# A recurrent attention with two feed-forward blocks on one core: a unit pattern made on chip, key loads of 48 rows, the last block's products in two parts, and another rank table

## The chip, the core and the metric

The kernel runs on one core of a Trainium2 chip. The time is device microseconds of one launch, from the core's own records. A change is called faster or slower here if the time moves by more than 2%.

## The reference

An attention with a recurrent 40x40 state for each of 4 x 8 heads over 768 steps, then two feed-forward blocks on its output (3072 tokens of 320 numbers). All is float32, and the kernel keeps float32 accuracy by taking most operands apart into a high and a low part.

```
for t in range(768):                       # for each batch b and head h
    y[t]  = r[t] @ state
    Sa    = state @ a[t]
    state = state * w[t] - outer(Sa, b[t]) + outer(v[t], k[t])
x = y as [3072, 320]
x = maximum(x @ w1, x @ w2, x @ w3) @ w_out        # inner width 768
x = ((x @ w_a) * (x @ w_b)) @ w_out2               # inner width 1536
```

## The kernel before

**Stages.** The 768 steps are cut into 24 chunks of 32 steps. In a chunk the recurrence becomes products of small matrices and one triangular solve. Two chunks make a pair, 12 pairs p in all. For each pair there are four pieces of work:

- prep(p) loads the decays (tile Wp), the keys k and b (KT) and a (ZL), makes running products of the decays by scans on VectorE (L484, L488), scales KT and ZL by them (L492, L504), multiplies them (L535 or L517), masks the product (L542), and writes it to memory (BD). From there it comes back in another layout (BU), the solve (L602, L603) builds the inverse in the tile TX of TXp, and TX goes out and comes back (TD, TT, L570 and L574).
- chain(c), one for each chunk, carries the state from chunk to chunk. In order: L723, the three or four small products L737, L750, L756 and L764, the new state L790 and L795, then the transposes L697 and the next chunk's L723. Beside it L680, L838 and L856 make the output y, which goes into XY.
- gather(p) writes XY to memory (XD, L870) and loads it as columns (xf, L875 and L877).
- moe_a(p) is the first feed-forward block on the 256 tokens of the pair (L964, L989 to L993). It needs xf and all first weights. Its results go to memory.

The first weights are loaded by weights_a in six blocks m, each of two raw loads (wraw, L897, 768 KB and 512 KB). VectorE turns the raw numbers into floats (L887 to L890). For m below 3 TensorE then makes the low parts (L917, L918, L920); these come in 18 groups of three steps. moe_b(n), six blocks of 512 tokens, is the second feed-forward block: for each of 12 slices ff there are two products of eight matmuls (L1111), a copy, a multiplication and a split into a high part bgh and a low part bgl (L1128 to L1132), and three products into each of four banks (L1119 to L1121). After the last slice the banks are copied out (L1139, L1141) and stored.

**What sets the order.** The kernel records each operation with the data that it reads and writes, and Plan.run lists them: at every step it takes the engine that can go on first and on it, of those that could start within 0.05 us, the operation of the least rank. It has estimated durations of its own. The rank is the operation's `pri`, less 0.04 times the length of the work behind it, plus a number out of the table RANK, which has one for each stage (c0 is the chain of chunk 0, p3 is prep(3), m, l, w and g the blocks, the weights and the gathers) and engine. So the table moves whole groups of operations on each engine. The order that comes out is fixed in the program: each engine runs its list in that order, and an instruction that waits holds all behind it. SP's list holds nearly all transfers. Where the plan leaves TensorE a gap of more than about 0.3 us it puts in 128x128 matmuls of a constant that nobody reads (L360, called fillers here; each is two instructions).

**What the change touches.** setup() zeroes tiles on VectorE and GpSimd at the start, and loads TXp, in which each 32-column row of TX begins with a row of a unit matrix, from an input `eye` of 128 x 528 (L439). load() in prep fills KT: for pairs 0 and 1 from a padded input `kb0` in pieces of 128 rows (L454), for the other ten with two loads of 48 rows each, at partitions 0 and 64 (L458). KT has two buffers, and later loads leave the padding rows alone.

Of the kernel before, what the change touches and what calls it, by code (L numbers as in the profile page):

```python
# [15 lines left out]
B, H, S, D = 4, 8, 768, 40  # L16
# [4 lines left out]
DM, DFF, DFF2 = 320, 768, 1536  # L21
NT = B * S
# [300 lines left out]
def body(nc, tc, ia, out_ap):  # L323
# [5 lines left out]
    op = P.op  # L329
# [90 lines left out]
    def setup():  # L420
# [18 lines left out]
        dma(lambda w_: SP.dma_start(TXp, ia["eye"]), 270e3, w=["TX"], pri=-0.55)  # L439


    def prep(p):
# [6 lines left out]
        def load(tile, name, n, nb, w, c0, c1):  # L449

            nb = nb * (c1 - c0) // 2
            if p < n:
                src = ia[name + "0"][p].rearrange("p (c f) -> p c f", c=2)
                dma(lambda w_: SP.dma_start(tile[:, c0:c1], src[:, c0:c1]), nb * 128, w=w(0) + w(1), pri=pr)  # L454
                return
            for g in range(2):
                src = ia[name][p, g].rearrange("p (c f) -> p c f", c=2)
                dma(lambda w_, g=g, src=src: SP.dma_start(tile[GP[g]:GP[g] + 48, c0:c1], src[:, c0:c1]), nb * 48, w=w(g), pri=pr)  # L458
# [852 lines left out]
def layout(d):  # L1311
# [18 lines left out]
    for n, m in (("kb", 2),):  # L1330
        z = np.zeros((m, 2, 64, o[n].shape[-1]), f)
        z[:, :, 0:D] = o[n][0:m]
        o[n + "0"] = z.reshape(m, 128, -1)
# [57 lines left out]
```

## Time and profile before

| | |
|---|---|
| median of 3 runs | 1036.34 us (1031.04 to 1044.56) |
| the profiled execution | 1038.84 us, its span 1037.1 us |
| TensorE busy | 1009.8 us, 97% of the span |
| VectorE, ScalarE, GpSimd busy | 627.5, 511.2, 125.7 us |
| transfers | 97.31 MB, 94 GB/s over the span |
| mean granted TensorE clock | 0.988 of full |

The span runs from the first to the last instruction of the profiled execution, and 1.7 us of its time lie outside. TensorE is the engine that is nearly always busy, but fillers count as busy too, so its share says nothing on how much of its work is wanted. The table of stretches has the busy time of each engine in 20 us, the clock that TensorE was granted as a share of full speed, and what the transfers moved. A piece of the chain of waits is what ended last at that time.

### The profile page before, as it was taken

To read this page: it belongs to the slowest core of one execution; us is meant where nothing else is said; L and a number is where in the kernel's file an instruction comes from. 1 tells how busy PE (TensorE), PEld (TensorE's weight loads), DVE (VectorE), ACT (ScalarE), POOL (GpSimd) and SP (SyncE) were. 2 spreads that over 40 slices of the span, in tenths; PEclk is the share of its full clock that TensorE was granted. 3 is DMA by queue.
4 is the path that set the end of the run, shared out by engine and by line. 5 is a ranking of instruction groups with operands and counts; after the bars stand their busy time and mean duration, and the time that the engine had idled before them with its cause. 6 is when DMAs were issued, how large, how long until landed. Compare 5 with 4: busy or idle time off the path is not lost.

```text
span 1037.1 us, 34548 instructions
## 1 busy us (share of the span) xinstructions
PE 1009.8 (97%) x15104; PEld 911.3 (88%) x15104; DVE 627.5 (61%) x1091; ACT 511.2 (49%) x1179; POOL 125.7 (12%) x128
## 2 busy tenths in 40 slices
PE   8999799999999999899999999999999999999997
PEld 8787698989999899899989999888888888888886
DVE  6787668968777788777866587773232232322222
ACT  4336668676786767667767244342232222322221
POOL 3100235205012123032111000000000000000000
PEclk9889999999999999999999999999999999999999
DMA  8946468575557457655463324312020000000000
GB/s 235 174 111 155 103 161 180 117 168 111 121 138 142 94 122 155 140 132 104 117 161 109 95 85 130 97 54 72 1 57 1 1 26 1 26 1 1 26 1 28
DMA packets 156397, 97.31 MB, mean 94 GB/s; under 512 B 120912, under 2 KB 135376, under 8 KB 155280
## 3 DMA queue, kind: packets, MB, share of 16 engines
q1 hardware_dynamic: 156096, 94.88, 38.7%
q8 instruction: 120, 1.97, 0.8%
q14 instruction: 37, 0.30, 0.1%
q10 hardware_dynamic: 144, 0.16, 0.0%
HBM read 76.26 MB, written 18.74 MB: 92 GB/s over the span
## 4 chain that ended last, share of the span: by engine, by line
PE 94%; DMA 2%; issue 2%; SPq 1%; DVE 1%; ACT 0%; POOL 0%; DVEq 0%
PE bank L1111 26%; PE bank L964 20%; PE bank L360 4%; PE bank L1120 4%; PE bank L1121 4%; PE bank L1119 4%; PE bank L856 3%; PE bank L838 2%; PE bank L989 2%; PE bank L723 2%; PE bank L737 2%; PE bank L680 2%; PE bank L790 2%; PE bank L535 2%; PE bank L990 2%
## 5 line engine op out<-in xcount | busy, mean ns | idle before, releaser
L1129 DVE TENSOR_TENSOR bas<-bank,bas 128x512 f32<-128x512 f32 x72 | 49.8, 691 | 195.5 <-PE bank L1111 187.3
L1131 ACT ACTIVATE bgh<-bas 128x512 fp32r<-128x512 f32 x72 | 45.5, 632 | 144.5 <-DVE bas L1129 144.5
L1128 ACT ACTIVATE bas<-bank 128x512 f32<-128x512 f32 x72 | 43.1, 598 | 121.6 <-PE bank L1111 121.6
L964 PE MATMUL bank<-xhi,whi 128*128 128x256 f32 x432 | 95.5, 303 | 0.0
L1111 PE MATMUL bank<-bxhi,bw 128*128 128x512 f32 x336 | 91.3, 393 | 0.0
L964 PE MATMUL bank<-xhi,wlo 128*128 128x256 f32 x432 | 87.1, 283 | 0.0
L964 PE MATMUL bank<-xlo,whi 128*128 128x256 f32 x432 | 86.9, 283 | 0.0
L1132 DVE TENSOR_TENSOR bgl<-bas,bgh 128x512 fp32r<-128x512 f32 x72 | 49.8, 692 | 42.5 <-ACT bgh L1131 42.3
L1111 PEld LDWEIGHTS bank<-bxhi,bw 128*128 128x128 f32 x336 | 61.9, 188 | 11.9
L964 PEld LDWEIGHTS bank<-xhi,whi 128*128 128x128 f32 x432 | 66.5, 191 | 3.3
L360 PE MATMUL bank<-con 128*128 128x128 f32 x442 | 65.4, 302 | 3.9 <-DMA con<-in_con_dram 3.0
L964 PEld LDWEIGHTS bank<-xhi,wlo 128*128 128x128 f32 x432 | 67.4, 191 | 0.1
L964 PEld LDWEIGHTS bank<-xlo,whi 128*128 128x128 f32 x432 | 67.2, 191 | 0.0
L1111 PE MATMUL bank<-bxhi,be 128*128 128x512 f32 x240 | 65.6, 395 | 0.0
L979 DVE TENSOR_TENSOR hm<-bank,hm 128x512 f32<-128x512 f32 x72 | 49.5, 688 | 26.1 <-PE bank L964 20.7
L360 PEld LDWEIGHTS bank<-con 128*128 128x128 f32 x442 | 59.4, 212 | 6.4 <-ACT bank L432 2.9
L964 PE MATMUL bank<-xt,wt 128*128 128x256 f32 x216 | 61.1, 283 | 0.0
L964 PE MATMUL bank<-xl,wt 128*128 128x256 f32 x216 | 60.8, 282 | 0.0
L780 ACT ACTIVATE XX<-bank 32x320 f32<-32x320 f32 x96 | 41.1, 429 | 23.3 <-PE bank L750 15.1
L1111 PE MATMUL bank<-bxlo,bw 128*128 128x512 f32 x168 | 52.4, 393 | 0.0
L1111 PEld LDWEIGHTS bank<-bxhi,be 128*128 128x128 f32 x240 | 44.2, 188 | 9.0
L1121 PE MATMUL bank<-bo,bgl 128*128 128x320 f32 x168 | 51.8, 309 | 0.0
(201 smaller groups left out, 2555.8 us busy)
## 6 DMA issues: line engine op xcount, KB each, us to landing
KT<-in_kb_dram SPq DMA_DIRECT2D x20, 384.0 KB
wraw<-in_wpa_dram SPq DMA_DIRECT2D x6, 768.0 KB
Wp<-in_wf_dram SPq DMA_DIRECT2D x20, 198.4 KB
ZR<-in_vz_dram SPq DMA_DIRECT2D x48, 80.0 KB
XX<-in_vx_dram SPq DMA_DIRECT2D x48, 80.0 KB
XT<-in_vt_dram SPq DMA_DIRECT2D x24, 160.0 KB
RB<-in_rb_dram SPq DMA_DIRECT2D x48, 80.0 KB
YL<-in_ry_dram SPq DMA_DIRECT2D x48, 80.0 KB
```

The costliest lines, as they stand in the source:

```text
L360: P.keep = lambda b: T.matmul(bank[b][:, 0:128], ident, ident, start=True, stop=True)
L780: own.append(op("ACT", ac(320), lambda w_, o_=o_, i_=i_: A.activation(o_(), i_(w_), AF.Copy), r=[pu], w=[("XXu", x, pq)], pri=pr))
L964: T.matmul(ps, w, x, start=(i == 0), stop=(i == 7))
L979: op("DVE", dv(512, True), lambda w_, pn=pn: V.tensor_tensor(f(hm), bank[w_[pn]], f(hm), ALU.max), r=[pn], w=["hm"], fin=[pn], pri=ep)
L1111: T.matmul(ps, w, x, start=(k == 0), stop=(k == 7))
L1119: T.matmul(o, gh[:, c], oh, start=ff == 0, stop=False)
L1120: T.matmul(o, gh[:, c], ol, start=False, stop=False)
L1121: T.matmul(o, gl[:, c], oh, start=False, stop=ff == 11)
L1128: op("ACT", ac(512), lambda w_, j=j, pa=pa: A.activation(tb["as", j], bank[w_[pa]], AF.Copy), r=[pa], w=[("bas", j)], fin=[pa], pri=ep)
L1129: op("DVE", dv(512, True), lambda w_, j=j, pb=pb: V.tensor_tensor(tb["as", j], bank[w_[pb]], tb["as", j], ALU.mult), r=[pb], w=[("bas", j) ...
L1131: op("ACT", ac(512), lambda w_, j=j, k=k: A.activation(tb["gh", k], tb["as", j], AF.Copy), r=[("bas", j)], w=[("gh", k)], pri=ep)
L1132: op("DVE", dv(512), lambda w_, j=j, k=k: V.tensor_tensor(tb["gl", k], tb["as", j], tb["gh", k], ALU.subtract), r=[("bas", j), ("gh", k)], ...
```

## The change

- setup() no longer loads `eye`: GpSimd zeroes TXp and writes ones over its diagonal with a stride of 33. Four new memsets on VectorE zero the two KT buffers, 128 x 1024 each.
- prep(0) and prep(1) load KT as the others do: eight pieces of 48 rows in place of four of 128.
- In moe_b the products of the very last slice are recorded as five operations: first those of bgh into all four banks, and then those of bgl one bank at a time.
- All numbers of RANK are others, so the order of everything moves.

```diff
 RANK = {
-    "ACT": 0.30, "DVE": -2.07, "POOL": 4.13, "SP": -3.60, "c0ACT": 6.38, "c0DVE": 3.21, "c0PE": -0.34, "c0SP": 6.32,
...
+    "ACT": -1.43, "DVE": 5.20, "POOL": -0.79, "SP": -5.70, "c0ACT": 3.50, "c0PE": -2.32, "c0SP": 5.63, "c10ACT": 6.01,
...
 }
...
-        dma(lambda w_: SP.dma_start(TXp, ia["eye"]), 270e3, w=["TX"], pri=-0.55)
+        zero(TXp, ["TX"], "POOL", pri=-2)
+        diag = TXp[:, 16:17]
+        op("POOL", 0.2, lambda w_: G.memset(bass.AP(tensor=diag.tensor, offset=diag.offset, ap=[list(diag.ap[0]), [33, 16]]), 1.0), w=["TX"], pri=-2)
+        for i in R2:
+            for c in R2:
+                op("DVE", 1.1, lambda w_, i=i, c=c: V.memset(KT[i][:, c].rearrange("p u x k s -> p (u x k s)"), 0.0), w=[(k, i, c, g) for k in ("K", "Kc") for g in R2], pri=-5.0 + i + 0.5 * c)
...
-        def load(tile, name, n, nb, w, c0, c1):
+        def load(tile, name, nb, w, c0, c1):
 
             nb = nb * (c1 - c0) // 2
-            if p < n:
-                src = ia[name + "0"][p].rearrange("p (c f) -> p c f", c=2)
-                dma(lambda w_: SP.dma_start(tile[:, c0:c1], src[:, c0:c1]), nb * 128, w=w(0) + w(1), pri=pr)
-                return
             for g in range(2):
                 src = ia[name][p, g].rearrange("p (c f) -> p c f", c=2)
                 dma(lambda w_, g=g, src=src: SP.dma_start(tile[GP[g]:GP[g] + 48, c0:c1], src[:, c0:c1]), nb * 48, w=w(g), pri=pr)
...
+            if n == NT // 512 - 1 and ff == 11:
+                def front(w_, k=k, ff=ff):
+                    for t in range(4):
+                        for q in range(2):
+                            T.matmul(bank[w_[po_[t]]][:, 0:DM], tb["gh", k][:, t * 128:t * 128 + 128], wb("bo", ff)[:, q], start=False, stop=False)
+
+                op("PE", 1.17, front, r=[("gh", k), ("bL", ff, 1)], w=po_, pri=pr)
+                for t in range(4):
+                    op("PE", 0.146, lambda w_, t=t, k=k, ff=ff: T.matmul(bank[w_[po_[t]]][:, 0:DM], tb["gl", k][:, t * 128:t * 128 + 128], wb("bo", ff)[:, 0], start=False, stop=True),
+                       r=[("gl", k), ("bL", ff, 1)], w=[po_[t]], pri=pr)
+                continue
```

The changed file has one line more from L483 on, so L897 before is L898 there, and L1121 is L1122.

**SP, the first transfers.** KT_119 and KT_120 are the two buffers of KT, and ZL_121, ZL_122 and ZL_123 are ZL of pairs 0, 1 and 2; wraw is raw first weights. Before:

```order
L427 DMA con<-in_con_dram 128x224
L439 DMA TXp<-in_eye_dram 128x528
L463 DMA Wp<-in_wf_dram 64x529 x4
L454 DMA KT_119<-in_kb_dram 128x1024 x2
L471 DMA ZL_121<-in_aa_dram 64x512 x4
L454 DMA KT_120<-in_kb_dram 128x1024
L463 DMA Wp<-in_wf_dram 48x529 x2
L454 DMA KT_120<-in_kb_dram 128x1024
L463 DMA Wp<-in_wf_dram 48x529 x2
L471 DMA ZL_122<-in_aa_dram 64x512 x4
```

Now:

```order
L427 DMA con<-in_con_dram 128x224
L898 DMA wraw<-in_wpa_dram 128x1536
L898 DMA wraw<-in_wpa_dram 128x1024
L472 DMA ZL_123<-in_aa_dram 64x2x512 x2
L464 DMA Wp<-in_wf_dram 64x529 x4
L459 DMA KT_119<-in_kb_dram 48x1024 x4
L472 DMA ZL_121<-in_aa_dram 64x512 x4
L662 DMA ZR_139<-in_vz_dram 32x640 x2
```

The two loads of weight block 0 and ZL of pair 2 now go ahead of the first decays and keys; before, `eye` did, and the first weights stood behind all of prep(0)'s and prep(1)'s loads. The raw load of block 2 now stands right behind the first half of BU in the same list, as the third of its size.

**VectorE, around the first solve** (the first L602 is the start of the solve of pair 0, and BU is its input). Before:

```order
L887 TENSOR_SCALAR wca<-wraw 128x512
L890 SCALAR_TENSOR_TENSOR wraw<-wraw,wca 128x768
L888 SCALAR_TENSOR_TENSOR wraw<-wraw,wca 128x512
L487 RECIPROCAL d_95<-Pp_128 128x16
L889 TENSOR_SCALAR wca<-wraw 128x512
L488 SCALAR_TENSOR_TENSOR Rr<-Wp,d_95 128x528
L602 TENSOR_TENSOR TP_152<-TXp,BU 128x2
L603 TENSOR_REDUCE TXp<-TP_152 128x2
L602 TENSOR_TENSOR TP_153<-TXp,BU 128x8
```

Now (one line later in the file: L603 and L604 are the solve):

```order
L888 TENSOR_SCALAR wca<-wraw 128x512
L889 SCALAR_TENSOR_TENSOR wraw<-wraw,wca 128x512
L890 TENSOR_SCALAR wca<-wraw 128x512
L891 SCALAR_TENSOR_TENSOR wraw<-wraw,wca 128x512
L543 TENSOR_TENSOR ZL_122<-bank_70,con 64x512
L888 TENSOR_SCALAR wca<-wraw 128x768
L493 TENSOR_TENSOR KT_120<-KT_120,Rr 128x1024
L603 TENSOR_TENSOR TP_152<-TXp,BU 128x2
L604 TENSOR_REDUCE TXp<-TP_152 128x2
L603 TENSOR_TENSOR TP_153<-TXp,BU 128x8
```

Before, the solve followed the second half of block 0's conversion and a scan. Now the first mask of the third weight block (L888 on 128x768) and a scaling of KT stand right ahead of it, and the conversions of blocks 0 and 1 further up.

**TensorE, the last products.** bank_70, 63, 67 and 68 before, and bank_64, 68, 66 and 69 now, take the outputs of the last 512 tokens. Before, the last two banks:

```order
L1119 MATMUL bank_67<-bo_10749,bgh_10159 128x320
L1120 MATMUL bank_67<-bo_10749,bgh_10159 128x320
L1121 MATMUL bank_67<-bo_10749,bgl_10160 128x320
L1119 MATMUL bank_68<-bo_10749,bgh_10159 128x320
L1120 MATMUL bank_68<-bo_10749,bgh_10159 128x320
L1121 MATMUL bank_68<-bo_10749,bgl_10160 128x320
```

Now:

```order
L1139 MATMUL bank_64<-bo_10801,bgh_10186 128x320 x2
L1139 MATMUL bank_68<-bo_10801,bgh_10186 128x320 x2
L1139 MATMUL bank_66<-bo_10801,bgh_10186 128x320 x2
L1139 MATMUL bank_69<-bo_10801,bgh_10186 128x320 x2
L1143 MATMUL bank_64<-bo_10801,bgl_10187 128x320
L1143 MATMUL bank_66<-bo_10801,bgl_10187 128x320
L1143 MATMUL bank_68<-bo_10801,bgl_10187 128x320
L1143 MATMUL bank_69<-bo_10801,bgl_10187 128x320
```

The four products of the low part come last, one for each bank, where each bank had its three products together. On TensorE the program as a whole now has 240 fillers instead of 221; 228 of them stand ahead of the first matmul of moe_a (the first L964, L965 now), where it was 209.

## Rows read from the trace of the kernel before

**Rows 1.** From the page: TensorE's busy share in 40 slices of the span.
```profile
PE   8999799999999999899999999999999999999997
```

**Rows 2.** Stretches: bounds, length, engines' busy us, clock, transfer share, GB/s.
```profile
0.00:20.00 20.00, 17.04 (x184) 16.78 (x186) 13.43 (x18) 12.45 (x28) 6.08 (x11) 1.00 0.89 237
20.00:40.00 20.00, 18.08 (x266) 16.60 (x264) 15.99 (x31) 3.50 (x9) 3.77 (x3) 0.83 0.85 170
60.00:80.00 20.00, 20.00 (x440) 16.12 (x439) 14.74 (x27) 9.99 (x29) 0.50 (x2) 0.83 0.45 114
100.00:120.00 20.00, 17.02 (x517) 14.85 (x516) 13.77 (x31) 13.42 (x35) 5.08 (x7) 1.00 0.33 82
120.00:140.00 20.00, 17.24 (x382) 15.70 (x382) 11.56 (x16) 10.96 (x29) 6.07 (x5) 0.83 0.75 173
420.00:440.00 20.00, 17.15 (x482) 15.40 (x469) 13.64 (x28) 14.43 (x38) 1.36 (x5) 1.00 0.63 144
```

**Rows 3.** Chain of waits to 175 us: start us, us, what.
```profile
58.81 0.68 PE bank L917 x2
...
62.15 0.72 PE bank L737 x64
...
85.92 1.35 PE bank L856 x64
87.27 0.86 PE bank L680 x8
...
94.06 0.72 PE bank L737 x64
...
150.60 1.08 PE bank L838 x32
151.68 1.25 PE bank L795 x4
152.94 0.71 PE bank L697 x8
153.65 0.73 PE bank L723 x62
154.38 1.14 PE bank L964 x8
```

**Rows 4.** Timeline to 45 us: start us, us, what [idle before, releaser].
```profile
5.61 1.26 DVE L484 TENSOR_TENSOR_SCAN Pp<-Wp,d 128x528 f32<-128x528 f32 x1 [4.03 <-DMA Wp<-in_wf_dram]
...
22.23 1.33 DVE L504 TENSOR_TENSOR ZL<-ZL,Pp 64x512 f32<-64x512 f32 x1 [1.67 <-DMA ZL<-in_aa_dram]
...
36.75 0.16 DVE L602 TENSOR_TENSOR TP<-TXp,BU 128x2 f32<-128x2 f32 x1 [1.80 <-DMA BU<-BD]
...
44.54 0.69 DVE L603 TENSOR_REDUCE TXp<-TP 128x64 f32<-128x512 f32 x1
```

**Rows 5.** VectorE's groups, 0 to 160 us: what, count | busy us, mean ns | idle.
```profile
L484 DVE TENSOR_TENSOR_SCAN Pp<-Wp,d 128x528 f32<-128x528 f32 x9 | 11.4, 1262 | 4.4 <-DMA Wp<-in_wf_dram 4.0 <-ACT d L481 0.2
...
L542 DVE TENSOR_TENSOR ZL<-bank,con 64x512 f32<-64x512 f32 x16 | 11.0, 688 | 5.9 <-PE bank L535 5.5
L492 DVE TENSOR_TENSOR KT<-KT,Rr 128x1024 f32<-128x1024 f32 x7 | 8.5, 1223 | 2.7 <-DMA KT<-in_kb_dram 2.6
...
L888 DVE SCALAR_TENSOR_TENSOR wraw<-wraw,wca 128x768 uint32<-128x768 uint32 x5 | 4.8, 953 | 0.3
L887 DVE TENSOR_SCALAR wca<-wraw 128x768 uint32<-128x768 uint32 x6 | 4.1, 686 | 4.1 <-DMA wraw<-in_wpa_dram 4.1
```

**Rows 6.** Timeline of the end.
```profile
1027.56 0.69 DVE L1132 TENSOR_TENSOR bgl<-bas,bgh 128x512 fp32r<-128x512 f32 x1 [0.70 <-ACT bgh L1131]
...
1029.43 0.31 PE L1119 MATMUL bank<-bo,bgh 128*128 128x320 f32 x1
...
1030.06 0.49 DVE L1141 COPY bos<-bank 128x320 f32<-128x320 f32 x1 [1.81 <-PE bank L1121]
...
1031.04 0.31 PE L1121 MATMUL bank<-bo,bgl 128*128 128x320 f32 x1
1031.38 0.44 ACT L1139 ACTIVATE bos<-bank 128x320 f32<-128x320 f32 x1 [0.44 <-PE bank L1121]
```

More of the change, by code (lines that the diff above doesn't have):

```diff
@@ L466, in prep @@
             cs = range(c0, c1)
-            load(K_.rearrange("p c u x k s -> p c (u x k s)"), "kb", 2, 8192, lambda g: [(k, kb_, c, g) for c in cs for k in ("K", "Kc")], c0, c1)
+            load(K_.rearrange("p c u x k s -> p c (u x k s)"), "kb", 8192, lambda g: [(k, kb_, c, g) for c in cs for k in ("K", "Kc")], c0, c1)
             for g in range(2):
@@ L1329, in layout @@
     o["wf"], o["wf0"] = np.ascontiguousarray(z[:, :, 0:48]), np.ascontiguousarray(z[0])
[L1330 to L1333, printed above, removed]
     z = np.zeros((NPB, 2, 64, 2, NU * C), f)
@@ L1342, in layout @@
     o["con"] = np.concatenate([np.eye(128, dtype=f), m0, np.where(np.arange(128)[:, None] // 32 % 2 == 1, -m0, m0), s == t], 1).astype(f)
-    o["eye"] = np.zeros((128, 528), f)
-    o["eye"][:, 16:].reshape(128, 16, 32)[:, :, 0:16] = np.eye(16, dtype=f)
     o["rb"] = np.ascontiguousarray(em(r)).reshape(NCH, 2, D, -1)
```

72 rows, old and new, of the table RANK are left out of this document.

## The prediction

> **What bounds it.** I read the busy shares over the span first. From the sixth tenth on TensorE is busy in every slice, and the gaps lie further ahead [rows 1]. That later part has the same matmuls in both programs, so the change can win time only at the start, lose it anywhere, and do a little at the very end. [...] Then I read the chain of waits up to the first matmul of moe_a, at 154.38 us [rows 3]. Ahead of it TensorE has only the first three chunks, the first weights and fillers, since moe_a(0) needs the output of two chunks and a way through memory. After it, wanted work always lies ready. So the time is near this: the first L964's time, plus the wanted work then left, plus the later stalls. Three marks cut the start: chunk 0's first small product (L737) at 62.15, chunk 1's at 94.06, the first L964 at 154.38.
>
> **To the first mark.** By the order SP's list up to BU, the input of the first solve, holds 7.36 MB before, and the solve starts on it at 36.75 us [rows 4]: 0.200 MB per us from zero on. In the new order the weights go ahead, `eye` is gone, and the first keys are 0.79 MB instead of 1.05. VectorE's first solve now stands behind the mask of weight block 2, whose raw load ends at 9.78 MB of the list. At 0.200 it lands at 48.9 us; at the two rates of the stretches [rows 2], at 41.3 and 57.5, which are my bounds. On VectorE follow the mask (0.69) and a scaling of KT (1.22) [rows 5], so that the solve starts at 50.8, 14 us later than before. It took 8.5 us, from 36.75 to the end of L603 at 45.23 [rows 4], and ends at 59.3. TensorE has the third block's first low part ahead of L738 (L737 before), and that waits for VectorE's ten operations behind the solve: three scans of 1.26, two of L542 with 0.69, two of the 768-wide conversions with 0.95, one of 0.69 [rows 5], and two reciprocals that I leave out: 7.75 us, to 67.0. The way of TD and TT lies beside that. Two TensorE steps of some 0.68 [rows 3] bring **68.4 us for the first mark**, against 62.15; bounds 60.8 and 77.0.
>
> **To the second mark.** Before, 31.9 us. By the order 13 of the 18 weight groups now stand ahead of the first mark, where it was 9, so four groups leave this stretch. A wide group is three steps of 0.68, narrower ones less; I take 1.25 each, 5.0 together. L680 (0.86) and chunk 0's L856 (1.35) leave it too [rows 3]. That gives 24.7 us if the stretch loses as much as before, and 21.3 if the 3.4 us of slow clock of 60 to 80 us [rows 2] don't come back. I take 23: 91.4 us.
>
> **To the third.** Before, 60.3 us. The new order adds here an L680 pair (0.86) and an L856 (1.35), and puts off until after the first L964 chunk 3's L838 (1.08), L795 (1.25), L697 (0.71) and the next L723 (0.73) [rows 3]: 58.8 us with the stalls of before. Without the idle 5.7 us and the slow 3.4 of 100 to 140 us [rows 2] it is 49.7. The new order also puts both halves of XD together and xf not far behind, where YL, ZL and weights stood between, so I take the middle, 54.2: **the first L964 at 145.6**, 8.8 us earlier. Of this 3.8 us are the four steps put off. What is won is **5.0 us**.
>
> **The other edits.** The four memsets of KT on VectorE cost nothing: VectorE is idle for 4.0 us ahead of 5.61 us, waiting for Wp [rows 4], and that transfer now comes later still; without this cover they would cost some 4 us at the rate of the other tiles zeroed. GpSimd's TXp is needed only by the solve. The four KT transfers more are issued while the queue has megabytes waiting. The 19 more fillers all lie ahead of the first L964 and fill waits that are in the marks already; after it there are 12 as before.
>
> **The end.** The split is meant for a wait that isn't there: the last low part is written from 1027.56 to 1028.25, and the last slice's products begin at 1029.43, TensorE being busy with older ones [rows 6]. The new order lets fewer products stand between, which the split makes harmless, but TensorE's own end doesn't move. What moves is the copies out. Before, bank 0's copy began at 1030.06, long ahead of the last at 1031.38, 0.34 us after the last matmul's start. Now all four banks are done within three steps of 0.146 us of each other. The two VectorE copies (0.49 each) and two ScalarE copies (0.44) queue: ScalarE's second ends 0.3 us later, VectorE's 0.5. I count **0.4 us lost**.
>
> **The sum** is -5.0 + 0.4 = -4.6 us. Against the profiled execution's 1038.84 us that is 1034.2. That execution is 2.5 us above the median of the runs, 1036.34, from which I forecast **1031.7 us**. With the middles of the two stretches moved to their ends this case runs from about 1025 to 1037. Chance 0.50.
>
> **Rivals.**
> - *The weights at the head hold up the start* (0.17). If the transfers run at the 170 GB/s of 20 to 40 us, block 2 lands at 57.5, the first mark is at 77.0 and the first L964 at 154.2, with 3.8 us of work put off and the 0.4: 1040.4. With the stalls of before in both stretches it is 160.5, and 1046.7. It decides from a first mark at 73.0 on, a landing at 53.5, or a rate under 183 GB/s. For it: more bytes ahead of the keys, and a solve that stands behind the third weight load. Against: 0.200 already contains that slow stretch.
> - *The gain is given back later* (0.13). A new order of everything meets other late transfers. In 420 to 440 us TensorE is idle for 2.85 us [rows 2]; two more such places would bring 1037.4. No row speaks for more or fewer of them.
> - *The start runs clean* (0.12). With the lower value in both stretches the first L964 comes at 139.4 and the time is 1025.5; at 237 GB/s besides, 7.6 us earlier still, 1018. Against: three chunks' waits for transfers are not gone because the order is another.
> - *A 48-row piece moves at half the rate* (0.08). The 1.57 MB of keys of pairs 0 and 1 would take as long as 3.15: 7.9 us more at 0.200, a first mark at 76.3, and 1039.6. For it: the second 20 us have more such narrow pieces and move 28% less in nearly the same busy share [rows 2]. Against: the first 20 us hold 64-row pieces too and reach 237.
>
> [...]
>
> **Numbers.** 2% is 20.7 us, about what a measurement of this kernel can tell from no change. Under 1015.6 lies only the far end of the clean start with fewer later stalls: 0.06. Above 1057.1 the slow start would need 10 us more than its dearest case: 0.03. The range of eight in ten reaches into both starts, 1018 to 1044.
>
> **What would show it.** In the changed profile: the first L603 near 51 us (at 58 the first rival, at 43 the third), and waiting for VectorE's line, not for BU; the first L738 near 68, the second near 91, the first L965 near 146; no idle VectorE time lost to the memsets; 240 fillers; TensorE busy in all slices from the sixth tenth on; the last copy out 0.3 us later behind TensorE's last matmul than before. I am wrong if the first L965 comes near 146 and the time does not follow, or if the marks move together by more than 8 us.

## The result, and the profile after

The change is **slower by 0.76%**: 1.0076 times the kernel before, interval 1.0052 to 1.0100, from 16 executions of each (medians 1037.59 and 1030.30 us). In a second set of runs it was 1.0070 (1.0042 to 1.0097). By the 2% rule that is no change, and the time lies in the forecast range; but the sign is the other one than forecast.

One thing has to be known to read the profiles. Executions of one kernel differ by 15 us and more here (the 16 of before lie between 1022.2 and 1044.6), and the two profiled ones stand at opposite ends: the one of before took 1038.84 us, where 118 later executions of it average 1027.9, and the one of after 1031.71, the third lowest of its 16. Left out of the 118 are three slow ones, over 1.5% above the fastest, and the profiled one of before is slow by the same measure. Laid side by side the two profiles show a gain of 7 us that is not there.

TensorE in 40 slices, and the clock it was granted (answers [rows 1]):

```profile
PE   8999899999999999999999999999999999999997
...
PEclk9997899999999999999999999999999999999999
```

The busy shares are much like those of [rows 1]; the clock has its deepest hole in the fourth slice. The stretches (answer [rows 2]; columns as there):

```profile
20.00:40.00 20.00, 20.00 (x328) 15.39 (x327) 17.20 (x25) 9.55 (x27) 0.00 (x0) 1.00 1.01 217
60.00:80.00 20.00, 20.00 (x353) 15.73 (x353) 17.76 (x34) 9.68 (x27) 1.52 (x1) 0.99 0.33 85
80.00:100.00 20.00, 20.00 (x490) 17.00 (x494) 9.10 (x16) 8.75 (x24) 4.28 (x3) 0.66 0.39 85
100.00:120.00 20.00, 18.48 (x498) 16.70 (x486) 17.89 (x34) 13.64 (x35) 7.19 (x7) 0.93 0.82 191
120.00:140.00 20.00, 17.86 (x395) 16.33 (x396) 12.11 (x15) 12.96 (x34) 2.65 (x3) 0.90 0.59 140
```

TensorE is no longer idle from 20 to 40 us, but from 80 to 100 us its mean clock is 0.66 (0.50 from 79.8 to 93.4 us), while it is busy all the time. The marks in the chain of waits (answer [rows 3]):

```profile
67.34 0.72 PE bank L738 x64
...
94.13 0.72 PE bank L738 x64
...
150.58 1.46 PE bank L965 x12
```

And VectorE ahead of the first solve (answers [rows 4]):

```profile
45.48 0.56 DVE L888 TENSOR_SCALAR wca<-wraw 128x768 uint32<-128x768 uint32 x1 [1.56 <-DMA wraw<-in_wpa_dram]
45.96 1.22 DVE L493 TENSOR_TENSOR KT<-KT,Rr 128x1024 f32<-128x1024 f32 x1
47.36 0.16 DVE L603 TENSOR_TENSOR TP<-TXp,BU 128x2 f32<-128x2 f32 x1 [0.18 <-DMA NB<-BD]
```

The solve stands behind the mask of weight block 2, as forecast, then waits 0.2 us for NB, and starts 10.6 us later than in [rows 4]. The end (answers [rows 6]):

```profile
1021.34 0.69 DVE L1133 TENSOR_TENSOR bgl<-bas,bgh 128x512 fp32r<-128x512 f32 x1 [0.70 <-ACT bgh L1132]
1021.44 1.36 PE L1139 MATMUL bank<-bo,bgh 128*128 128x320 f32 x8
1022.64 0.75 PE L1143 MATMUL bank<-bo,bgl 128*128 128x320 f32 x4
1022.98 0.89 DVE L1153 COPY bos<-bank 128x320 f32<-128x320 f32 x2 [0.95 <-PE bank L1143]
1023.28 0.77 ACT L1151 ACTIVATE bos<-bank 128x320 f32<-128x320 f32 x2 [1.97 <-PE bank L1143]
```

The low part's products begin 0.6 us behind the low part and wait for nothing. The copies queue: the last ends at 1024.05, 0.97 us after the last matmul's start at 1023.08 (1022.64 and three steps of 0.146), where it was 0.78.

### The profile page after: what moved, and what is told of

Its sections match the earlier page's. It is cut to its first block, busy times and chain, and to the rows that moved or that the text cites. A ratio compares the mean times of both kernels' runs of the same rounds, so it can differ in the third digit from the quotient of the medians.

```text
span 1029.8 us, 34646 instructions
## 1 busy us (share of the span) xinstructions
PE 1010.0 (98%) x15142; PEld 911.4 (89%) x15142; DVE 630.2 (61%) x1095; ACT 510.8 (50%) x1179; POOL 128.8 (13%) x130
## 4 chain that ended last, share of the span: by engine, by line
PE 96%; DMA 1%; issue 1%; ACT 1%; DVE 0%; SPq 0%; DVEq 0%; ACTq 0%
PE bank L1112 26%; PE bank L965 21%; PE bank L360 6%; PE bank L1122 4%; PE bank L1121 4%; PE bank L1120 4%; PE bank L857 3%; PE bank L839 3%; PE bank L536 2%; PE bank L990 2%; PE bank L681 2%; PE bank L724 2%; PE bank L738 2%; PE bank L698 2%; PE bank L791 2%; PE bank L992 2%
## 5 line engine op out<-in xcount | busy, mean ns | idle before, releaser
L1132 ACT ACTIVATE bgh<-bas 128x512 fp32r<-128x512 f32 x72 | 45.5, 632 | 167.6 <-DVE bas L1130 167.6
L965 PE MATMUL bank<-xhi,whi 128*128 128x256 f32 x432 | 95.0, 301 | 0.2 <-ACT YR L688 0.2
L965 PE MATMUL bank<-xhi,wlo 128*128 128x256 f32 x432 | 86.9, 283 | 0.0
L965 PE MATMUL bank<-xlo,whi 128*128 128x256 f32 x432 | 86.9, 283 | 0.0
L965 PEld LDWEIGHTS bank<-xhi,whi 128*128 128x128 f32 x432 | 66.5, 191 | 3.7 <-ACT YR L688 0.4
L965 PEld LDWEIGHTS bank<-xlo,whi 128*128 128x128 f32 x432 | 67.1, 191 | 0.0
L965 PEld LDWEIGHTS bank<-xhi,wlo 128*128 128x128 f32 x432 | 67.1, 191 | 0.0
L965 PE MATMUL bank<-xt,wt 128*128 128x256 f32 x216 | 61.1, 283 | 0.0
L965 PE MATMUL bank<-xl,wt 128*128 128x256 f32 x216 | 60.8, 282 | 0.0
L1120 PE MATMUL bank<-bo,bgh 128*128 128x320 f32 x164 | 50.6, 308 | 0.0
```

The source lines that it names most:

```text
L965: T.matmul(ps, w, x, start=(i == 0), stop=(i == 7))
L1120: T.matmul(o, gh[:, c], oh, start=ff == 0, stop=False)
L1132: op("ACT", ac(512), lambda w_, j=j, k=k: A.activation(tb["gh", k], tb["as", j], AF.Copy), r=[("bas", j)], w=[("gh", k)], pri=ep)
```

## Experiments

Two kinds. In rank_only, edits_only, old_start, no_split and split_only the planner orders the altered program anew. In those that are called *order kept*, the planner's finished list stays as it is but for the edit, so that every other instruction keeps its place on its engine.

### Table and edits apart, planned anew

**rank_only**: before with the new RANK. **edits_only**: the change with the old RANK.

> The kernel before with the new rank table alone (eye loaded, 128-row keys, products of the last slice together). The change measured 1.0076 times before, some 8 us. Theory A, the order loses: 1.005 to 1.010 here too, since the table moves everything and the three edits only some microseconds. Theory B, the edits at the start lose (more narrow key loads, memsets ahead of the first work): 1.000 or under, and the first L737 well ahead of the change's 67 us. My forecast's own view would be 0.99 to 1.00, with the first L964 near 145 to 150 us. A table made for the changed program may also not suit this one: over 1.010 would say so.

> The changed kernel with the rank table of before: eye made on chip, eight 48-row key loads, split last products. Theory A, the order loses: 0.998 to 1.003, the first L738 near the 62 us of before. Theory B, the edits lose: 1.005 to 1.010, the first L738 some microseconds later than 62.

Measured: rank_only 1.0129 (1.0090 to 1.0169); edits_only **1.0639** (1.0587 to 1.0691), which neither theory allows. Its plan has 441 fillers, where before has 221. In its profile TensorE does this in front of the last block of moe_a:

```profile
644.14 1.42 PE L857 MATMUL bank<-YL,YR 128*40 128x32 f32 x64
645.49 12.77 PE L360 MATMUL bank<-con 128*128 128x128 f32 x112
658.02 0.48 PE L965 MATMUL bank<-xhi,whi 128*128 128x256 f32 x2
```

12.8 us of nothing but fillers, put there by the planner itself, which by its estimated durations had no wanted work ready there. So a table of this kind belongs to one list of operations: each of the two programs is slow under the other's, and this comparison says nothing on what an edit costs.

**old_start**: the new table and the split, with the old loads of eye and keys. **no_split**: the change with l4 in one piece again (the planned order is the same until late in moe_a).

```diff
-            if n == NT // 512 - 1 and ff == 11:
...
-                continue
```

> The new table and the split, but eye loaded and keys of pairs 0 and 1 in 128-row pieces, as before. Theory A, the order loses: like the change, 1.005 to 1.010. Theory B, the start's edits lose: 1.000, and the first key products earlier than in the change.

> The changed kernel with the last slice's products in one piece again; the order of the middle moves a little with it. If the split costs what I counted (0.4 us at the end) this is 1.007 times before, no different from the change in any measurement of this size, and from TensorE's last matmul to the last copy's end it takes 0.3 to 0.5 us less. If the split mattered for the 8 us it would be within 1.002 of before.

Measured: old_start 1.0104 (1.0076 to 1.0132), which for the same reason decides nothing. no_split 1.0078 (1.0054 to 1.0103): the split is not the loss. Its last copy ends 0.79 us after the last matmul's start, against 0.97.

### Was the base odd?

**before_again**, **after_again** and **after_third** are the two kernels unchanged.

> The kernel before, unchanged, for a second profile: the one that the forecast rests on took 1038.84 us, with a granted clock of 0.988, where the median of the runs taken since is 1028 to 1030 at 0.993. From the first moe_a matmul to the end the profiles so far take 879 to 883 us whatever the kernel. Theory A, the base was an odd execution: its three stretches of 6.8 us at half clock ahead of the first L964 are not the rule; the first L964 then comes at 144 to 148 us instead of 154.38, and the time is 1025 to 1032. Theory B, the start is what it was and the later part varies: the first L964 at 153 to 156 again, and the remainder 872 to 876.

> The changed kernel, unchanged, for a second profile: the first is of an execution of 1031.71 us where the median is 1037.59, and has its first L965 at 150.40. Theory A: the time varies with the start, so an execution near the median has its first L965 at 153 to 157 and 879 to 883 us behind it. Theory B: the first L965 near 150 in every execution, and a remainder of 884 to 888 us near the median.

> The changed kernel once more, for the profile of an execution near its median (1034.8 to 1037.6): the profiles of its order so far are of executions that took 1026 to 1034 us. If an ordinary execution loses its time ahead of the first moe_a matmul: the first L965 at 152 to 156 us, with two or more falls of the clock ahead of it, and 879 to 882 us from there to the end. If it loses it later: the first L965 at 143 to 151 and more than 883 us behind it.

Measured: before_again 1.0013 (0.9985 to 1.0042), its profiled execution 1031.5 us. Its marks, from the timeline of TensorE:

```profile
58.01 0.79 PE L737 MATMUL bank<-Zs,TT 32*32 32x40 f32 x64
...
147.78 0.50 PE L964 MATMUL bank<-xhi,whi 128*128 128x256 f32 x2
```

4 and 6.5 us ahead of [rows 3]. Theory A holds, at the edge of its 144 to 148; four more kernels in this order are below. after_again took 1033.9 us with its first L965 at 150.91, which is neither of its theories clean: the mark is earlier than A said, and the 881.2 us behind it are A's. after_third, 1034.35 us, came as an ordinary execution should by the expectation that the start loses it: first L965 at 153.01 and 879.6 behind it. The profiles of the two kernels and of six others in one of the two orders (128-row keys in the changed order are further down), each mark read from the timeline of TensorE, "half clock" being the time at a granted clock of 0.5 ahead of the third mark:

| kernel | first L737 | second chunk | first L964 | half clock | from there to the end |
|---|---|---|---|---|---|
| *order of before* | | | | | |
| the base | 62.1 | 94.0 | 154.3 | 20.5 | 882.7 |
| before_again | 58.0 | 88.4 | 147.8 | 10.2 | 881.9 |
| split_only | 58.1 | 86.9 | 142.8 | 0 | 884.1 |
| keys48_before | 56.7 | 88.6 | 142.2 | 6.8 | 880.3 |
| edits_in_order | 57.2 | 88.0 | 143.6 | 3.4 | 888.4 |
| fill_before | 59.7 | 88.5 | 142.3 | 3.4 | 884.7 |
| *order of the change* | | | | | |
| the change | 67.3 | 94.1 | 150.4 | 20.5 | 879.4 |
| after_again | 74.1 | 94.8 | 150.9 | 13.7 | 881.2 |
| after_third | 70.5 | 97.3 | 153.0 | 23.9 | 879.6 |
| no_split | 67.7 | 88.4 | 143.4 | 3.4 | 880.7 |
| fill_after | 70.6 | 91.3 | 146.9 | 6.8 | 881.0 |

The base is alone: the other five have their first L964 at 142.2 to 147.8, 143.7 on the mean. Only the latest of them, before_again, is the kernel before without any edit.

The table does not say what sets the first mark in the order of the change. In no_split (TensorE, and then VectorE's last step on the first half of weight block 2):

```profile
51.71 13.39 PE L360 MATMUL bank<-con 128*128 128x128 f32 x118
64.94 0.84 PE L918 MATMUL bank<-wraw,con 128*128 128x384 f32 x2
...
66.94 0.83 PE L360 MATMUL bank<-con 128*128 128x128 f32 x6
67.70 0.79 PE L738 MATMUL bank<-Zs,TT 32*32 32x40 f32 x64
...
59.73 0.91 DVE L891 SCALAR_TENSOR_TENSOR wraw<-wraw,wca 128x768 f32<-128x768 uint32 x1
```

59 fillers (118 instructions) stand in a row ahead of that block's first low part, L918. VectorE has its numbers ready at 60.64; L918 begins at 64.94, and TensorE is not idle in between. In all five profiles of this order L918 begins 2.6 to 7.5 us behind these numbers, and from 45 us to the first mark TensorE is never idle but for 3.0 us in after_again. So the first mark comes when TensorE's own list has got to it, fillers included, at the clock granted. Up to the first L965 fillers take 62.3 to 63.5 us of TensorE in this order, and 55.8 to 59.8 us in before's (the base, 61.2, and the two runs with fillers put in aside).

### The edits in before's order

**split_only** is planned anew (the same order up to late in moe_a); **keys48_before** (48-row keys and the memsets) and **edits_in_order** (all three edits) keep the order.

```diff
-                dma(lambda w_: SP.dma_start(tile[:, c0:c1], src[:, c0:c1]), nb * 128, w=w(0) + w(1), pri=pr)
+                def both(w_):
+                    for g in range(2):
+                        sg = ia[name][p, g].rearrange("p (c f) -> p c f", c=2)
+                        SP.dma_start(tile[GP[g]:GP[g] + 48, c0:c1], sg[:, c0:c1])
...
+                dma(both, nb * 128, w=w(0) + w(1), pri=pr)
```

> The kernel before with the last slice's products split, and nothing else; the order is that of before up to row 2134 of TensorE's list, late in the first feed-forward block. If the split costs what I counted, 1.000 to 1.001. From the start of the last matmul to the end of the last copy out it should be 0.3 to 0.5 us longer than before's 0.78. If it were a gain as it is meant, 0.999, and no queue of copies.

> The kernel before with its order kept, but each of the four 128-row key loads of pairs 0 and 1 as two 48-row pieces, and the four memsets of KT on VectorE at the start. The changed kernel with 128-row pieces took 0.9953 of the change. If narrow pieces (or their four issues more on SP's list) are the cause, 1.002 to 1.005 of before here, with the first scalings of KT (9.3 to 9.7 us before) some us later. If what that run gained hangs on the change's order, 0.999 to 1.001.

> The kernel before with its order kept instruction for instruction and all three edits put in where they stand: unit pattern by two memsets on GpSimd and no load of eye, 48-row keys with the four memsets of KT, and the last slice's products as eight of the high and then four of the low part. The edits under before's table, with the order planned anew, were 1.0639; here the table and the order are out of it. If the edits themselves cost nothing, as I counted but for 0.4 us: 0.998 to 1.002, and the whole loss of the change is its order. If they are part of its 0.75%: 1.003 or more.

Measured: 1.0011 (0.9986 to 1.0036), 1.0010 (0.9985 to 1.0034) and 1.0030 (1.0001 to 1.0059). split_only's last copy ends 0.97 us after its last matmul's start, 0.2 us more than before's 0.78, where its expectation gave 0.3 to 0.5. In keys48_before the first scaling of KT is not late; the third line is that of before:

```profile
5.85 1.26 DVE L489 TENSOR_TENSOR_SCAN Pp<-Wp,d 128x528 f32<-128x528 f32 x1
...
8.73 1.23 DVE L497 TENSOR_TENSOR KT<-KT,Rr 128x1024 f32<-128x1024 f32 x1
...
9.68 1.23 DVE L492 TENSOR_TENSOR KT<-KT,Rr 128x1024 f32<-128x1024 f32 x1 [1.23 <-DMA KT<-in_kb_dram]
```

It starts at 8.73, right behind the scan that feeds it (7.43 and 1.26 long), so it waits for no keys; the base waits 1.2 us for its 128-row keys, until 9.7, and before_again 1.0, until 9.3. The edits together cost some 3 us in this order, hardly clear of nothing; the rest lies with the new order, or with an edit that costs more in it.

### 128-row keys in the changed order

**keys128_fixed** (no memsets of KT), **keys128_memset** (with them), and the first again for a profile, **keys128_third**; order kept.

```diff
             for g in range(2):
+                if p < 2:
+                    s0 = ia[name + "0"][p].rearrange("p (c f) -> p c f", c=2)
+                    dma((lambda w_, s0=s0: SP.dma_start(tile[:, c0:c1], s0[:, c0:c1])) if not g else (lambda w_: None), nb * 48, w=w(g), pri=pr)
+                    continue
```

> The changed kernel with its order kept instruction for instruction, but keys of pairs 0 and 1 loaded as 128-row pieces from the padded input (one for two 48-row ones) and without the four memsets of KT. It moves 0.52 MB more. If narrow pieces move at half the rate, the start's transfers end up to 5 us earlier than in the change and it is 0.995 to 0.998 of the change's time (1.003 of before). If they don't matter, as I gave it 0.92, it is like the change, 1.006 to 1.009 of before.

> The changed kernel, order kept, with 128-row key loads for pairs 0 and 1 but with its four memsets of KT. With the same loads and without the memsets it took 1.0028 of before, the change 1.007 on the same chip; 48-row pieces in before's order cost nothing that can be measured. If the pieces cost in this order: 1.003 again. If the memsets did: 1.007. If the 4 us were chance: between, 1.004 to 1.007.

> The changed kernel with its order kept and 128-row key loads, without memsets of KT, for a third profile: the two so far have the first L738 at 67.1 and 67.7 us, where those with 48-row pieces have 67.3, 67.7, 70.6 and 74.1. If the pieces matter there: 67 to 68 again. If the spread is chance, it can be anywhere from 67 to 74.

Measured: 1.0028 (1.0005 to 1.0052) and 1.0027 (0.9992 to 1.0062), against 1.0070 for after_again, timed beside the first, and 1.0066 for fill_after, beside the second. So the memsets cost nothing that can be told, and wide pieces in this order look some 4 us better. Only the first of the two comparisons is clear of noise (3.6 us between the means, give or take 2.4), and fill_after is not quite the change, since it has 13 fillers more. The edit also makes one load of two, so it does not tell the width of a piece from the number of loads. How it gains is not shown. The keys themselves are no earlier: this is keys128_fixed, and the change has the same scaling at 13.65.

```profile
13.91 1.23 DVE L497 TENSOR_TENSOR KT<-KT,Rr 128x1024 f32<-128x1024 f32 x1
```

keys128_third has its first L738 at 67.6, so the three wide profiles have 67.1 to 67.7, and the five narrow ones 67.3 to 74.1: the expectation that the pieces matter there is met, on few profiles. Their first L965 stand at 149.7, 144.6 and 144.5, within the 143.4 to 153.0 of the narrow ones.

### What stands ahead of the first solve

**weights_head**: before, order kept, with the two raw loads of weight block 0 moved to the head of SP's list, as in the change. **solve_first**: the change, order kept, with the second raw load of block 1 and the first of block 2 moved behind BU and NB, and the work on them behind the first solve. **solve_first_wide**: that with 128-row keys.

```diff
+    raw = [x for x in L if x[0] == "w0" and x[1] == "SP"]
+    rest = [x for x in L if x not in raw]
+    k = next(n for n, x in enumerate(rest) if x[1] == "SP") + 1
+    return rest[:k] + raw + rest[k:]
```

> The kernel before with its order kept, but the two raw loads of weight block 0 (1.31 MB) moved from behind the loads of prep(0) and prep(1) to the head of SP's list, right behind con, as in the change. In the change the first decay scan starts at 10.8 us and not at 5.6, with these loads ahead. If the weights at the head are what makes it slower: the first scan at 9.5 to 11, the first solve some 4 to 5 us later than the 35 to 37 us of before, and 1.002 to 1.005 of before. If the start absorbs it (the first moe_a matmul waits for something else): the same late scan, but 1.000 within 0.001.

> The changed kernel with its order kept but for one thing: the second raw load of weight block 1 and the first of block 2 go behind BU and NB on SP's list, and the operations on them behind the first solve on VectorE, TensorE and ScalarE. In the change the load of block 1 waits for TensorE (3.7 and 7.4 us in the two profiles) with BU behind it, and VectorE's mask of block 2 waits 1.6 and 3.2 us with the solve behind it. If these waits make the change slow: the first solve at 42 to 44 us instead of 47.4 and 49.4, no idle TensorE near 46 us, and 1.002 to 1.005 of before. If the start is paced elsewhere: 1.007 as the change.

> solve_first and the 128-row key loads (without memsets of KT) together. If both are real and independent, their gains add: 0.998 to 1.001 of before. If the 128-row pieces only helped because the late weight load came earlier, it is like the better of the two alone, 1.002 to 1.004.

Measured: weights_head **1.0045** (1.0016 to 1.0074), with the scan where the expectation had it:

```profile
10.56 1.26 DVE L495 TENSOR_TENSOR_SCAN Pp<-Wp,d 128x528 f32<-128x528 f32 x1 [8.98 <-DMA Wp<-in_wf_dram]
```

VectorE waits 8.98 us for the decays, which come behind 1.31 MB of weights; before it was 4.03 [rows 4]. The first solve starts at 38.9, the first mark is at 62.1 and not at 57 to 60, the first moe_a matmul at 148.8. One move of the many in the table makes a loss of 0.45% in before's order, over half of the 0.76% sought, though its interval allows a fifth of it.

solve_first came out the other way, **1.0177** (1.0136 to 1.0218), and solve_first_wide 1.0175 (1.0137 to 1.0213). The solve did start a little earlier, at 45.6, but the weights had kept TensorE busy. Stretches of solve_first:

```profile
40.00:46.00 6.00, 6.00 (x101) 5.86 (x100) 2.55 (x5) 1.45 (x4) 0.00 (x0) 1.00 0.83 140
46.10:53.70 7.60, 0.00 (x0) 0.00 (x0) 7.05 (x18) 0.00 (x0) 0.00 (x0) 0.64 0.60 176
53.70:68.70 15.00, 14.94 (x51) 10.74 (x52) 11.45 (x17) 3.78 (x12) 1.17 (x1) 0.50 0.24 62
68.70:75.00 6.30, 6.30 (x58) 6.30 (x58) 6.00 (x14) 1.45 (x4) 0.00 (x0) 1.00 0.59 127
```

TensorE does nothing for 7.6 us, and then its low parts run at half clock for 15 us. The first L738 comes at 81.7. My theory that the waits at these two loads make the change slow falls: they cost little beside what their work covers.

### Fillers at the waits

**fill_before** puts 21 more fillers ahead of four products that TensorE waits for, **fill_after** 13 ahead of two; order kept.

```diff
+            for _ in range({631: 4, 1047: 8, 2205: 5, 2706: 4}.get(x[2], 0)):
+                out.append(("keep", "PE", -1, lambda w_, b=x[5]: self.keep(b), None, None))
+            out.append(x)
```

> The kernel before with its order kept and 21 more fillers, put right ahead of four products that TensorE waits 1 to 2.6 us for in most profiles (the fourth L723, the seventh and seventeenth run of L790, the 22nd of L737). Behind the waits of some 2 us the granted clock falls to half for 3.4 or 6.8 us. If an idle TensorE is what lets the clock fall there, no fall at 200 to 207 us, the mean clock rises from 0.993 to 0.995 and the time is 0.996 to 0.999 of before. If the falls come from elsewhere, or the fillers delay what they precede (21 of 0.28 us are 5.9 us in all): 1.000 to 1.005.

> The changed kernel with its order kept and 13 more fillers, three ahead of the third run of L738 and ten ahead of the third of L765, where TensorE is idle for 2.1 to 3.9 us at 114 to 125 us in all four profiles with that order, and the clock then falls for 3.4 us. If the idle time makes the fall: none there, and some 2 us less than the change, 1.005. If not: 1.007 or more, since 3.6 us of fillers stand in the way.

Measured: 0.9989 (0.9956 to 1.0022) and 1.0066 (1.0032 to 1.0101): no gain that can be told, and no loss by the fillers put in. In fill_before the mean granted clock is 0.995 where 32 executions of before beside it have 0.993, as its expectation had it; that rise is not clear of noise either. In both profiles the clock holds where the fillers stand, at 198 to 212 us and at 112 to 128:

```profile
198.00:212.00 14.00, 13.24 (x285) 11.62 (x284) 10.03 (x18) 11.27 (x30) 1.56 (x1) 1.00 0.70 173
```

```profile
112.00:118.00 6.00, 5.73 (x164) 5.26 (x163) 5.80 (x7) 2.39 (x6) 5.41 (x4) 1.00 0.90 157
118.00:128.00 10.00, 7.55 (x178) 6.97 (x177) 6.38 (x9) 4.00 (x10) 0.00 (x0) 1.00 0.81 211
```

In before_again the clock falls to 0.51 at 206.9 us for 3.4, which costs 1.7 us; fill_before has no fall there, but others of the same length at 243 and 417 us, and a mean clock of 0.994 in its profiled execution. In fill_after TensorE is still idle for 2.5 us of 118 to 128, in shorter waits. None of the versions is clearly faster than before.

## Why the prediction was wrong

- **The step that failed is the base of the sum:** "Against the profiled execution's 1038.84 us" with its marks 62.15, 94.06 and 154.38, and "2.5 us above the median of the runs". The ordinary first L964 is at 143.7 (five profiles), 10.6 us ahead of the base's. [Rows 2] showed why: three stretches with a mean clock of 0.83. I read them as what the kernel loses and a new order might win; they were what that one execution had lost: 20.5 us at half clock ahead of the mark, where the other five have 0 to 10.2. The kernel before already has the clean start that I forecast for the changed one. And the base stood 11 us above the later mean of 1027.9, not 2.5.
- **A second step failed beside it,** the term put at nothing: "The 19 more fillers all lie ahead of the first L964 and fill waits that are in the marks already". In the new order TensorE is never idle from 20 us to the second mark, but for 3.0 us in after_again, and 59 fillers in a row hold up work that is ready. At full clock 19 fillers take 4.3 us (59 take 13.39 in no_split), an estimate. No run takes fillers out, so what they cost is not shown; the 21 and 13 that were put in ahead of waits cost nothing that can be told.
- **The first solve and the first mark** came near the forecast by luck. The solve was forecast at 50.8, behind the load of block 2; it started at 46.1 to 49.4 in the five narrow profiles of the new order, and only in three of them does VectorE wait for that load (1.6 to 3.2 us). The first L738 was forecast at 68.4 and measured at 67.3 to 74.1, but not by the path forecast: VectorE had the numbers for the low part ready at 60.6 to 63.9 and not at 67.0, and TensorE was still in its fillers.
- **The second stretch** was near in both of its cases: 21.3 us if the slow clock does not come back and 24.7 if it does, 23 taken; measured 20.7 in three profiles and 26.8 in two, those with a fall of 13.7 us at 80 to 97 us, where the forecast had 6.8.
- **The third stretch** was forecast at 54.2 and measured at 55.0 to 56.3. The first L965 came at 148.9 on the mean instead of 145.6: 1.6 us by the first mark, 0.1 by the second stretch and 1.5 by the third.
- **Work put off and the end** were right on the mean: -3.8 and +0.4 us forecast, together -3.4; from the mark to the end the five profiles of the new order take 880.4 us on the mean and those of the old order, the base aside, 883.9, with a spread of 8 us among these. The queue of copies costs 0.2 us (0.97 against 0.78), not 0.4.
- **So the sign.** Against the ordinary 143.7 the new mark is 5.2 us later, not 8.8 earlier, and 3.5 are given back. The 1.7 us left are less than the 8 measured, since the profiled executions of the new order average 1031.1 us and the means of its timed ones lie between 1034.7 and 1037.5. Of that gap the clock is a part, and for the rest no profile caught such an execution.
- **The clock's share** can be estimated from the runs alone, taking (1 - granted clock) x 1030 us as full-speed time lost. In the set that timed both kernels side by side, 34 executions of before lose 6.8 us on the mean, and 11 of the change 10.0: 3.2 of the 7.6 us between their means, 1027.1 and 1034.7. What is left over, 4.4 us, is not the clock; it is near the 4.3 us of 19 fillers. weights_head loses 9.8 us in this way against 6.4 for the 23 executions of before beside it, so 3.3 of the 5.2 us between their means. rank_only and old_start lose no more to the clock than before and are 14.1 and 11.6 us slower; they have 251 fillers ahead of the first L964, where before has 209. That fits fillers as a cost, but a plan that expects more waits also has more fillers.
- **The first rival,** that the weights at the head hold up the start, named a place that does cost in before's order (weights_head), but its mechanism did not come: it needed a first mark at 73 from slow transfers, and the mark stayed at 67 to 71 in four of five profiles, with block 2 waited for until 45.5 us in the change and not 57.5.
- **Narrow pieces.** The last rival gave a 48-row piece half the rate. Neither order shows it: KT is scaled at 8.73 with 48-row pieces against 9.3 and 9.7 with 128-row ones, and at 13.65 against 13.91. No run times one piece alone. The 4 us that wide pieces seem to gain in the changed order remain without a shown cause.
- **The split** meets no wait of its own in the old order, as forecast, and costs nothing that can be told: 1.0011, and no_split like the change.

Open: which rows of the table besides the weights' place cost time, since the table can't be changed in part without a new plan, and what the new order would take with fewer fillers. That the larger part of the loss goes with the new order is the reading of edits_in_order (0.30% of the 0.76%, though its interval reaches to 0.59%); which part of the order makes it is shown for the weights' place alone, and there in before's order.

## What to carry to other kernels

Before a forecast is set against a profiled execution, compare its time and granted clock with the other executions: where runs differ by 15 us, a stall in one profile is a stall of the kernel only if a second one has it. Undo an edit with the instruction order held fixed; a planner's table that was fitted to one list of operations made the other list look bad, both ways round. Where an engine's list is filled up with unwanted work, count that work as work: once the engine is never idle, the list itself is the path. And before work is moved away from ahead of a wait, ask what it covered.

## What the hardware showed that I had not expected

What stood behind a short wait of TensorE cost more than the wait. In after_again it waits for a scaling of KT that stands behind a late weight load:

```profile
47.79 0.56 DVE L888 TENSOR_SCALAR wca<-wraw 128x768 uint32<-128x768 uint32 x1 [3.17 <-DMA wraw<-in_wpa_dram]
...
49.54 0.67 PE L536 MATMUL bank<-ZL,KT 40*64 40x32 f32 x15 [3.01 <-DVE KT L493]
```

3.0 us idle, and then 10.2 us at half clock, by (1 - granted clock) 5.1 us of full speed:

```profile
46.50:49.50 3.00, 0.03 (x1) 0.00 (x0) 1.71 (x3) 0.00 (x0) 0.00 (x0) 1.00 0.56 111
50.40:60.60 10.20, 10.20 (x77) 8.89 (x74) 9.69 (x19) 2.88 (x10) 1.18 (x1) 0.50 0.34 89
```

That execution has the latest first mark of the five, 74.1. In the profile of before TensorE has single waits of 1.92, 2.45 and 2.21 us from 25.3, 125.7 and 210.1 us on, and its clock is 0.51 to 0.52 from 28.7 to 35.5, 127.6 to 134.4 and 213.0 to 216.4; in that of the change one of 2.14 from 122.3 on, and a clock of 0.50 from 124.1 to 127.5. That the wait brings the fall is not shown, and the clock also fell with no idle time right ahead: in before at 66.2 us (0.51 to 73.0), with TensorE busy for all of 60 to 80. In after_third TensorE is busy for all of the 8.4 us before a fall of 13.7, mostly with products of 32 to 64 rows:

```profile
75.00:83.40 8.40, 8.40 (x161) 6.37 (x161) 3.92 (x6) 4.44 (x12) 1.50 (x1) 1.00 0.30 98
83.40:97.10 13.70, 13.70 (x246) 11.44 (x245) 7.41 (x13) 4.23 (x10) 3.69 (x2) 0.50 0.26 61
97.10:100.00 2.90, 2.90 (x140) 2.55 (x139) 0.36 (x1) 2.56 (x11) 0.00 (x0) 1.00 0.61 167
```

no_split has the same instructions there and no fall: its second mark is at 88.4, that of after_third at 97.3. What makes the difference is not shown. It is worth 6.1 us of the second stretch (26.8 against 20.7), about as much as the whole spread of the first mark.
